# The order in which TensorE reads its streamed operand, mixed by block, in a fused attention and MLP kernel

## The chip, the cores and the metric

The kernel runs on one core of one Trainium2 chip. The metric is the device time of one execution in microseconds; a smaller number is better. Three runs of the kernel before gave a median of 866.39 us (864.64 to 867.66).

## The reference

What is computed, cut to the arithmetic, with its shapes:

```python
# q, k, v: (8, 8, 576, 64) float32;  g_norm: (64,)
kv  = np.einsum('bhsd,bhse->bhde', k, v)
out = np.einsum('bhsd,bhde->bhse', q, kv)
rms = np.sqrt(np.mean(out * out, axis=-1, keepdims=True) + 1e-06)
x   = (out / rms * g_norm).transpose(0, 2, 1, 3).reshape(4608, 512)
# w_in: (512, 2048), w_out: (2048, 512) float32
h = x @ w_in
g = np.maximum(h, 0.0) + np.log1p(np.exp(-np.abs(h)))     # softplus
return g @ w_out                                           # (4608, 512)
```

The attention is small. Nearly all work lies in the two large products, `x @ w_in` and `g @ w_out`.

## The kernel before

**Three products for one.** Inputs are float32, but TensorE reads them here as `float32r`. To keep the accuracy, each operand is split into three parts (a high part, a scaled low part and a third one that mixes both), and each large product is done as three matmuls that accumulate in the same place of `banks`, the PSUM tile. In the code `m` counts the three parts.

**Two stages.** The hidden width of 2048 is cut into 16 chunks of 128. A first stage does chunks 0 to 3 for the first four blocks of tokens, and 0 to 5 for the other eight; a block has 384 tokens, and there are 12 blocks (`n` in `step`). A wide stage does the other chunks in pairs, on blocks of 512 tokens (nine of them, `n` in `wide_step`), in two passes `ph` = 1 and 2. The list `STEPS` holds its 48 steps.

- In `step`, `mm1` (line 863) does the 12 matmuls of one chunk's first product: three parts by four blocks of the contraction (`kd`), each streaming 384 columns of `xv`. ACT takes the softplus and splits it with DVE. `mm2` (line 870) does the second product, for each of three tiles of tokens three matmuls that stream 512 columns of `w_out`.
- In `wide_step`, a pair of chunks is done by a scheme of seven half-size products instead of eight (`PRODUCTS`, functions `product` and `multiply`). Each of the seven visits has six matmuls (line 1065), three parts by two `kd`, that stream 256 columns of `dst`. The second product, `mm2` (line 1136), is done in eight visits of three matmuls that stream 512 columns of `outs[c]`.

**What sets the order.** `Plan` writes the order out ahead of time: each task carries an estimated duration and a position, and `Plan.order` places the tasks on the engines. A visit (one `product`, one `mm2`) is one task, so its matmuls follow each other on PE. The visits of L1065 and L1136 are interleaved in the wide stage, those of L863 and L870 in the first one. The plan knows nothing of the order in which a matmul reads its columns.

**The order of reading.** `from_the_end` (line 42) rewrites an operand of N columns as N/4 blocks of 4 columns, last block first. In the kernel before it is used in `product` alone, for the streamed operand and for the output in `banks`, so that each column still lands in its place. The other three lines read and write their columns in ascending order.

Of the kernel before, what the change touches and what calls it, by code (L numbers as in the profile page):

```python
# [9 lines left out]
F32R = mybir.dt.float32r  # L10
# [8 lines left out]
P = 128  # L19
# [19 lines left out]
    return x.rearrange(f"r ({' '.join(names)}) -> r {' '.join(names)}", **dict(zip(names, shape[1:])))  # L39


def from_the_end(x):

    return x.rearrange("p (b w) -> p b w", w=4)[:, ::-1]


class Slot:
# [13 lines left out]
class Plan:  # L61
# [19 lines left out]
    def slot(self, ring):  # L81
        return Slot(ring)

    def add(self, engine, ns, run, after=(), pos=0.0, take=(), give=(), size=0, behind=None, follows=None, kind="all"):
        pos, behind = round(pos, 4), None if behind is None else round(behind, 4)
        t = Task(engine, ns, run, [a for a in after if a is not None], pos, list(take), list(give), size)
        for s in t.give:
            s.readers += 1
        self.tasks.append(t)
        t.follows = follows  # L90
        t.behind = behind
        t.kind = kind
        return t
# [113 lines left out]
def kernel(  # L207
# [24 lines left out]
    nc = tc.nc  # L232
# [5 lines left out]
    KD, KF = d_model // P, d_ff // P  # L238
    NT = 384
    TB = NT // P  # L240
# [12 lines left out]
    LAST = 2  # L253
# [595 lines left out]
    def step(s):  # L849
        n, c = ORDER[s]  # L850
        cs = CHUNKS[n]
        h, g, gv = slot("h"), slot("g"), slot("gv")
        if c == cs[0]:
            sums[:] = [slot(f"s{i}") for i in range(TB)]
        xv, w_in, w_out = xv_slots[n], w_slots[0, c], w_slots[1, c]
        mine = list(sums)
        kept = c >= 4

        def mm1():
            hp = new(h, [P, NT])  # L860
            for m in range(3 * KD):
                i, kd = divmod(m, KD)
                nc.tensor.matmul(hp, lhsT=w_in.tile[:, i, kd * P:(kd + 1) * P], rhs=xv.tile[:, i, kd],  # L863
                                 start=(m == 0), stop=(m == 3 * KD - 1))

        def mm2(i):
            if c == cs[0]:
                new(mine[i], [P, d_model])
            for m in range(3):
                nc.tensor.matmul(mine[i].tile, lhsT=gv.tile[:, m, i * P:(i + 1) * P], rhs=w_out.tile[:, m],  # L870
                                 start=(c == cs[0] and m == 0), stop=(c == cs[-1] and m == 2))

        def low():
            nc.vector.tensor_tensor(out=gv.tile[:, 1], in0=g.tile, in1=gv.tile.bitcast(F32)[:, 0], op=ALU.subtract)

        def less():
            f32 = gv.tile.bitcast(F32)
            nc.vector.scalar_tensor_tensor(out=gv.tile[:, 2], in0=f32[:, 1], scalar=-RADIX, in1=f32[:, 0],
                                           op0=ALU.mult, op1=ALU.add)

        a = add("PE", 2100, mm1, x_split[n] + factors_done[0, c] + [m for _, m in mm1s[-1:]] +
                (factors_done[1, ORDER[s - 2][1]] if s > 1 else []), s, [h],
                ([xv] if c == cs[-1] else []) + ([w_in] if s == last_step[c] and c != 4 else []))
        mm1s.append((s, a))
        a = add("ACT", 490, lambda: nc.scalar.activation(new(g, [P, NT]), h.tile, func=AF.Softplus, scale=1.0 + E),  # L885
                [a], s, [g], [h])
        a = add("ACT", 530, lambda: nc.scalar.activation(new(gv, [P, 3, NT], F32R)[:, 0], g.tile, func=AF.Copy, scale=DOWN),
                [a], s, [gv])
        a = add("DVE", 570, low, [a], s, [], [g])
        a = add("DVE", 570, less, [a], s)  # L890
        for i in range(TB):
            a2 = add("PE", 700, lambda i=i: mm2(i), [a] + factors_done[1, c] + [mm2s.get(i)], s + 1.5,
                     [mine[i]] if c == cs[0] else [],
                     [gv] + ([w_out] if s == last_step[c] and not kept else []))
            mm2s[i] = a2
            if c == cs[-1]:
                leave(0, n * TB + i, mine[i], a2, s + 1.5)
# [145 lines left out]
    def wide_step(k):  # L1043
        ph, n, p = STEPS[k]
        ab, gv = slot("ab"), slot("gvp")
        b = starts[k]
# [3 lines left out]
        mine = list(wide_sums)  # L1050
        outs = [w_slots[1, c] for c in (2 * p, 2 * p + 1)]

        def place(q):
            return ab.tile[:, q // 2, q % 2 * HW:(q % 2 + 1) * HW]
# [3 lines left out]
        def product(u, q):  # L1058
            f, i = PRODUCTS[u]
            w = forms[p][f].tile  # L1060
            dst, v = unit_slots[ph, n, u]
            for m in range(3):
                for kd in range(2):
                    at = i * 2 * P + kd * P
                    nc.tensor.matmul(from_the_end(place(q)), lhsT=w[:, m, at:at + P],  # L1065
                                     rhs=from_the_end(dst.tile[:, m, v, kd] if u < 6 else dst.tile[:, m, kd]),
                                     start=(u == 0 and not m and not kd), stop=(m == 2 and kd == 1), skip_group_check=True)

        def multiply(u, q, after, pos, take=(), follows=None):
            f = PRODUCTS[u][0]  # L1070
            give = [unit_slots[ph, n, u][0]] if last else []
            if final and u in (2, 3, 5, 6):
                give.append(forms[p][f])
            return add("PE", 710, lambda: product(u, q), unit_done[ph, n, u] + forms_done[p][f] + list(after), pos, take, give,
                       follows=follows)
# [3 lines left out]
        def gt(dtype=F32):  # L1079
            if dtype not in held:  # L1080
                held[dtype] = sb.tile([P, 2, WIDE], dtype, tag=f"g{gv.place}", name=f"g{gv.place}_{dtype == F32}")
            return held[dtype]

        def gvt(m, dtype=F32):
            y = gv.tile[:, m]
            return y if dtype == F32R else y.bitcast(F32)
# [8 lines left out]
        def begin():  # L1095
            new(ab, None)
            product(0, X)
# [33 lines left out]
        def mm2(c, i):  # L1131
            fresh = first and not c and ph < LAST
            if fresh:
                new(mine[i], [P, d_model])
            for m in range(3):
                nc.tensor.matmul(mine[i].tile, lhsT=(gvt(m, F32R) if m < 2 else gt(F32R))[:, c, i * P:(i + 1) * P], rhs=outs[c].tile[:, m],  # L1136
                                 start=fresh and not m, stop=(last and c == 1 and m == 2), skip_group_check=True)

        seeds = {}
# [19 lines left out]
        for c in range(2):  # L1159
            for i in range(TW):  # L1160
                slot_pos = b + PACE + MM2[TW * c + i]
                a2 = add("PE", 700, lambda c=c, i=i: mm2(c, i),
                         [split_done[c]] + factors_done[1, 2 * p + c] + ([seeds[i]] if i in seeds and not c else []) +
                         ([before[i]] if c or not first else []), slot_pos, [mine[i]] if first and not c and ph < LAST else [], [gv] + ([outs[c]] if final else []))
                before[i] = a2
                if last and c:
                    leave(ph, TW * n + i, mine[i], a2, slot_pos)
# [98 lines left out]
```

## Time and profile before

| What | Value |
|---|---|
| median of 3 runs | 866.39 us (864.64 to 867.66) |
| the profiled execution | 864.34 us, its span 862.5 us |
| granted TensorE clock, mean | 0.999 |
| PE busy | 849.7 us, 99% of the span |
| DVE busy | 704.6 us, 82% |
| L1065, products of the wide stage | 2016 matmuls of 256 columns |
| L1136, second side of the wide stage | 1152 matmuls of 512 columns |
| L863, first product of the first stage | 768 matmuls of 384 columns |
| L870, second product of the first stage | 576 matmuls of 512 columns |

Times are of one profiled execution unless a row says otherwise. A matmul's record begins where it starts and ends where its last result is modelled to land; the records overlap, so that the distance from one start to the next is what a matmul costs in a row of them, not the length of its record. PEld is the load of the weights, which runs beside the matmuls.

### The profile page before, as it was taken

Reading aid. Unit: us, or ns where it says so; the run is one execution under the profiler, and the core shown is the slowest. Engines: PE = TensorE matmul, PEld = TensorE weight load, DVE = VectorE, ACT = ScalarE, POOL = GpSimd, SP = SyncE. Lnnn points to the kernel's source line nnn. Section 1 sums busy time; section 2 is a strip of 40 time slices with the busy share of each in tenths; the row PEclk is TensorE's granted clock in tenths of the full one; section 3 lists DMA queues with packets and bytes.
Section 4 is the critical chain, followed back from the end, with each engine's and each line's share of the span. In section 5 each row is a group of like instructions: output and inputs, shape, how many; then the busy total and the mean of one; then the engine's idle time right before and its main releaser. Section 6 shows DMA issues by size and latency. Waiting matters only on the chain.

```text
span 862.5 us, 17080 instructions
## 1 busy us (share of the span) xinstructions
PE 849.7 (99%) x6464; PEld 757.7 (88%) x6464; DVE 704.6 (82%) x995; ACT 521.2 (60%) x980; POOL 76.1 (9%) x79
## 2 busy tenths in 40 slices
PE   8899999999999999999999999999999999999998
PEld 5578888898888999999999999998999899999996
DVE  7988898888788888798888788878788766788873
ACT  6866664436354467766667665654868555566654
POOL 0342223111113300000000000000000000000000
PEclk9999999999999999999999999999999999999999
DMA  9998997779784655436645546645364753778863
GB/s 285 283 234 222 261 263 242 178 235 226 210 188 118 188 157 183 141 107 216 199 158 164 166 154 205 190 158 176 123 196 138 232 165 102 244 234 240 247 187 130
DMA packets 239778, 167.07 MB, mean 194 GB/s; under 512 B 106320, under 2 KB 198736, under 8 KB 239696
## 3 DMA queue, kind: packets, MB, share of 16 engines
q1 hardware_dynamic: 239392, 165.86, 65.7%
q8 instruction: 50, 0.82, 0.4%
q14 instruction: 32, 0.26, 0.1%
q10 hardware_dynamic: 304, 0.13, 0.1%
HBM read 112.98 MB, written 52.95 MB: 192 GB/s over the span
## 4 chain that ended last, share of the span: by engine, by line
PE 94%; DVE 1%; ACT 1%; POOL 0%; issue 0%; ACTq 0%; DVEq 0%
PE banks L1136 30%; PE banks L1065 28%; PE banks L870 16%; PE banks L863 15%; PE banks L720 2%; PE banks L696 2%; PE banks L738 0%; DVE units L643 0%; DVE half L732 0%; PE banks L1230 0%; POOL roots L728 0%; DVE units L646 0%; DVE roots L724 0%; DVE m L464 0%; ACT units L640 0%
## 5 line engine op out<-in xcount | busy, mean ns | idle before, releaser
L1136 PE MATMUL banks<-pieces,gv 128*128 128x512 f32 x768 | 238.0, 391 | 0.0
L1136 PE MATMUL banks<-pieces,g_False 128*128 128x512 f32 x384 | 149.4, 389 | 0.0
L1136 PEld LDWEIGHTS banks<-pieces,gv 128*128 128x128 f32 x768 | 132.5, 188 | 17.3
L863 PE MATMUL banks<-units,pieces 128*128 128x384 f32 x768 | 145.4, 337 | 0.0
L870 PE MATMUL banks<-pieces,gv 128*128 128x512 f32 x576 | 144.9, 396 | 0.0
L863 PEld LDWEIGHTS banks<-units,pieces 128*128 128x128 f32 x768 | 135.5, 188 | 4.9
L870 PEld LDWEIGHTS banks<-pieces,gv 128*128 128x128 f32 x576 | 106.1, 188 | 20.3
L1065 PEld LDWEIGHTS banks<-units,pieces 128*128 128x128 f32 x840 | 112.0, 188 | 6.5 <-ACT banks L1111 0.4
L1065 PE MATMUL banks<-units,pieces 128*128 128x256 f32 x840 | 116.4, 282 | 0.0
L885 ACT ACTIVATE half<-banks 128x384 f32<-128x384 f32 x64 | 31.5, 492 | 97.3 <-PE banks L863 97.1
L1126 DVE TENSOR_TENSOR gv<-g_True,gv 128x1024 fp32r<-128x1024 f32 x47 | 57.5, 1224 | 36.5 <-ACT gv L1123 36.5
L1136 PEld LDWEIGHTS banks<-pieces,g_False 128*128 128x128 f32 x384 | 72.1, 188 | 15.7
L1065 PEld LDWEIGHTS banks<-units,w 128*128 128x128 f32 x504 | 67.3, 188 | 3.7 <-ACT banks L1111 0.2
L1065 PE MATMUL banks<-units,w 128*128 128x256 f32 x504 | 70.3, 282 | 0.0
L728 POOL TENSOR_TENSOR roots<-roots,half 128x8 f32<-128x8 f32 x36 | 62.2, 1727 | 3.0
L1129 DVE SCALAR_TENSOR_TENSOR g_False<-gv 128x1024 fp32r<-128x1024 f32 x47 | 57.6, 1225 | 1.5
L1028 DVE TENSOR_TENSOR units<-loads,units 128x1024 fp32r<-128x1024 f32 x42 | 51.2, 1219 | 6.2 <-ACT units L1025 6.1
L1093 ACT ACTIVATE g_True<-banks 128x256 f32<-128x256 f32 x96 | 36.7, 383 | 31.6 <-PE banks L1065 31.0
L1115 DVE TENSOR_TENSOR g_True<-banks,g_True 128x512 f32<-128x512 f32 x48 | 33.2, 691 | 27.7 <-PE banks L1065 22.5
L930 ACT ACTIVATE m<-banks 128x512 f32<-128x512 f32 x72 | 42.1, 595 | 18.7 <-PE banks L1136 12.8
L1031 DVE SCALAR_TENSOR_TENSOR units<-units 128x1024 fp32r<-128x1024 f32 x42 | 51.4, 1224 | 1.8
L1025 ACT ACTIVATE units<-loads 128x1024 fp32r<-128x1024 f32 x42 | 44.5, 1059 | 12.4 <-PE banks L1065 8.9
(115 smaller groups left out, 1250.2 us busy)
## 6 DMA issues: line engine op xcount, KB each, us to landing
loads<-x SPq DMA_DIRECT2D x180, 128.0 KB, 2.7
part<-m SPq DMA_DIRECT2D x72, 256.0 KB, 2.9
m<-part SPq DMA_DIRECT2D x72, 256.0 KB, 3.3
loads<-form SPq DMA_DIRECT2D x45, 256.0 KB, 3.3
form<-loads SPq DMA_DIRECT2D x36, 256.0 KB, 3.1
raw<-in_moe_w_in_dram SPq DMA_DIRECT2D x16, 512.0 KB, 4.8
loads<-in_k_dram SPq DMA_DIRECT2D x32, 256.0 KB, 4.4
loads<-in_v_dram SPq DMA_DIRECT2D x32, 256.0 KB, 4.6
```

Source lines behind the costliest of these rows:

```text
L728: nc.gpsimd.tensor_tensor(out=r.tile, in0=r.tile, in1=half, op=ALU.pow)
L863: nc.tensor.matmul(hp, lhsT=w_in.tile[:, i, kd * P:(kd + 1) * P], rhs=xv.tile[:, i, kd], start=(m == 0), stop=(m == 3 * KD - 1))
L870: nc.tensor.matmul(mine[i].tile, lhsT=gv.tile[:, m, i * P:(i + 1) * P], rhs=w_out.tile[:, m], start=(c == cs[0] and m == 0), stop=(c == cs ...
L930: a = add("ACT", 690 if ph == LAST else 600, lambda: nc.scalar.activation(new(ot, [P, d_model]), bank.tile, func=AF.Copy, scale=scale if p ...
L1025: nc.scalar.activation(part_of(0, F32R), xl.tile if m > 1 else xl.tile[:, 0], func=AF.Copy, scale=DOWN)
L1028: nc.vector.tensor_tensor(out=part_of(1, F32R), in0=xl.tile if m > 1 else xl.tile[:, 0], in1=part_of(0), op=ALU.subtract)
L1031: nc.vector.scalar_tensor_tensor(out=part_of(2, F32R), in0=part_of(1), scalar=-RADIX, in1=part_of(0), op0=ALU.mult, op1=ALU.add)
L1065: nc.tensor.matmul(from_the_end(place(q)), lhsT=w[:, m, at:at + P], rhs=from_the_end(dst.tile[:, m, v, kd] if u < 6 else dst.tile[:, m, kd ...
L1093: nc.scalar.activation(dst, src, func=AF.Softplus, scale=1.0 + E)
L1126: nc.vector.tensor_tensor(out=gvt(1, F32R), in0=gt(), in1=gvt(0), op=ALU.subtract)
L1129: nc.vector.scalar_tensor_tensor(out=gt(F32R), in0=gvt(1), scalar=-RADIX, in1=gvt(0), op0=ALU.mult, op1=ALU.add)
L1136: nc.tensor.matmul(mine[i].tile, lhsT=(gvt(m, F32R) if m < 2 else gt(F32R))[:, c, i * P:(i + 1) * P], rhs=outs[c].tile[:, m], start=fresh ...
```

## The change

`from_the_end` takes the length `w` of the blocks; a length of 0 leaves the operand in ascending order. Four tables give the lengths, block by block:

- `SHORT[ph][n]`: for the six matmuls of each product visit, taken in turn. `(8, 16)` means blocks of 8 in the first, 16 in the second, 8 in the third and so on. Where all six had blocks of 4, they now have pairs, triples or one list of six lengths out of 0, 1, 2, 4, 8, 16, 32, 64 and 128.
- `LONG[n]`: for the three matmuls of a visit of the wide stage's `mm2` in pass 2: blocks of 128, none, 256, or 128 and none in turn. In pass 1 all are read in blocks of 128 from the end.
- `FIRST_SHORT[n]`: for the first and the last of the 12 matmuls of `mm1` in the first stage. The ten between stay in ascending order.
- `FIRST_LONG[n]`: for the very last matmul of a chunk's `mm2` in the first stage.

```diff
-def from_the_end(x):
-    return x.rearrange("p (b w) -> p b w", w=4)[:, ::-1]
+def from_the_end(x, w):
+    return x.rearrange("p (b w) -> p b w", w=w)[:, ::-1] if w else x
+
+SHORT = {1: [(8, 16), (16, 8, 4), (16, 8, 8), (16, 16, 8), (32, 8), (64, 8), (64, 16), (8, 1), (8, 2)],
+         2: [(128, 8), (128, 16), (16, 8, 16, 4, 16, 2), (8, 4, 16), (16, 1, 8), (16, 8), (16, 8), (16, 8), (0, 8)]}
+LONG = [(128,), (128,), (128,), (128,), (128,), (0,), (256,), (128, 0), (128,)]
+FIRST_SHORT = [(0, 0)] + [(0, 1)] * 7 + [(1, 1), (4, 1), (16, 1), (0, 2)]
+FIRST_LONG = [0, 0, 1, 4, 16, 8, 128, 64, 0, 0, 0, 2]
...
 # step, mm1
-                nc.tensor.matmul(hp, lhsT=w_in.tile[:, i, kd * P:(kd + 1) * P], rhs=xv.tile[:, i, kd],
+                w = FIRST_SHORT[n][1] if m == 3 * KD - 1 else 0 if m else FIRST_SHORT[n][0]
+                nc.tensor.matmul(from_the_end(hp, w), lhsT=w_in.tile[:, i, kd * P:(kd + 1) * P], rhs=from_the_end(xv.tile[:, i, kd], w),
...
 # step, mm2
-                nc.tensor.matmul(mine[i].tile, lhsT=gv.tile[:, m, i * P:(i + 1) * P], rhs=w_out.tile[:, m],
+                w = FIRST_LONG[n] if i == TB - 1 and m == 2 else 0
+                nc.tensor.matmul(from_the_end(mine[i].tile, w), lhsT=gv.tile[:, m, i * P:(i + 1) * P], rhs=from_the_end(w_out.tile[:, m], w),
...
 # wide_step, product
-                    nc.tensor.matmul(from_the_end(place(q)), lhsT=w[:, m, at:at + P],
-                                     rhs=from_the_end(dst.tile[:, m, v, kd] if u < 6 else dst.tile[:, m, kd]),
+                    t = SHORT[ph][n][(2 * m + kd) % len(SHORT[ph][n])]
+                    nc.tensor.matmul(from_the_end(place(q), t), lhsT=w[:, m, at:at + P],
+                                     rhs=from_the_end(dst.tile[:, m, v, kd] if u < 6 else dst.tile[:, m, kd], t),
...
 # wide_step, mm2
-                nc.tensor.matmul(mine[i].tile, lhsT=(gvt(m, F32R) if m < 2 else gt(F32R))[:, c, i * P:(i + 1) * P], rhs=outs[c].tile[:, m],
+                t = LONG[n][m % len(LONG[n])] if ph == LAST else P
+                nc.tensor.matmul(from_the_end(mine[i].tile, t), lhsT=(gvt(m, F32R) if m < 2 else gt(F32R))[:, c, i * P:(i + 1) * P],
+                                 rhs=from_the_end(outs[c].tile[:, m], t),
```

## The prediction

> **What bounds the kernel now.** I read the page from the top: busy shares, the chain that ended last, and then the waits of PE.
>
> ```profile
> span 862.5 us, 17080 instructions
> PE 849.7 (99%) x6464; PEld 757.7 (88%) x6464; DVE 704.6 (82%) x995; ACT 521.2 (60%) x980; POOL 76.1 (9%) x79
> ...
> PE 94%; DVE 1%; ACT 1%; POOL 0%; issue 0%; ACTq 0%; DVEq 0%
> PE banks L1136 30%; PE banks L1065 28%; PE banks L870 16%; PE banks L863 15%; PE banks L720 2%; PE banks L696 2%; PE banks L738 0%; DVE units L643 0%; DVE half L732 0%; PE banks L1230 0%; POOL roots L728 0%; DVE units L646 0%; DVE roots L724 0%; DVE m L464 0%; ACT units L640 0%
> ```
>
> The chain is PE for 94% of the span, and four lines hold 89% of it: the two sides of the wide stage (L1136, L1065) and the two of the first stage (L870, L863). These are exactly the four lines that the change edits. The windows by stage say the same:
>
> ```profile
> core 0: us, PE busy (x) PEld busy (x) DVE busy (x) ACT busy (x) POOL busy (x), PEclk, DMA share, GB/s
> 0.00:42.00 42.00, 34.40 (x434) 24.20 (x437) 35.20 (x64) 29.90 (x58) 8.98 (x15) 1.00 1.00 284
> 42.00:338.00 296.00, 294.52 (x2775) 261.76 (x2775) 253.71 (x435) 162.59 (x321) 67.14 (x64) 1.00 0.77 206
> 338.00:862.00 524.00, 520.78 (x3265) 471.73 (x3263) 415.68 (x498) 328.73 (x603) 0.00 (x0) 1.00 0.58 180
> ```
>
> After 42 us PE is idle for under 5 us of 820, the granted clock is 1.00, and the next engine, DVE, is busy 254 of 296 us and 416 of 524 us. So a nanosecond off a matmul's spacing moves the end, up to many microseconds, and so does one added. The question is only what an order of reading does to that spacing. A busy PE hides it, because the records of matmuls overlap; the starts show it:
>
> ```profile
> start us, us, engine line op out<-in xcount [idle before <-releaser]
> ...
> 599.74 0.88 PE L1065 MATMUL banks<-units,w 128*128 128x256 f32 x6
> 600.45 0.62 PE L1136 MATMUL banks<-pieces,gv 128*128 128x512 f32 x2
> 600.90 0.39 PE L1136 MATMUL banks<-pieces,g_False 128*128 128x512 f32 x1
> 601.13 0.62 PE L1136 MATMUL banks<-pieces,gv 128*128 128x512 f32 x2
> ```
>
> Six 256-column products take 600.45 - 599.74 = 0.71 us, 118 ns each; three 512-column ones 601.13 - 600.45 = 0.68 us, 227 ns each. The median records are 281, 334 and 389 ns for 256, 384 and 512 columns (L1065, L863, L1136), that is (389 - 281) / 256 = 0.42 ns per column. A column at that price makes 108, 162 and 216 ns; each matmul thus carries a gap of about 10 to 12 ns on top. That gap is all that an order can win: 10 ns on 2016 products and 11 ns on some 1100 long ones, 32 us at the very most.
>
> **What the trace says of the gap.** Start to start, from the start times of single records:
>
> - L863, read forward, settles at 173.4 ns; but behind L870 it begins 171, 175, 178, 185, 176, 181, 174. That is 26 ns more over seven.
> - L870, forward, settles at 227; behind L863 it begins 229, 233, 236, 224, 231, 236, 228, 233, 230, 37 ns more over nine.
> - L1136, forward: 226.9 when settled, 228.2 on average inside a visit; some visits begin 235, 231 behind L1065.
> - L1065, read from the end in blocks of 4: mean 118.5. The second, fourth and sixth intervals of a visit average 116.4; the first, third and fifth 120.2, alternating between 118 and 123.
>
> The gap is therefore not a constant: it is smallest in half of the intervals of the one line that is read backwards (116.4 - 108 = 8.4 ns, against 11 forward), and it swings for several matmuls when the shape changes. Both are small.
>
> **The change part by part.** The matmuls, their order, weights, outputs and waits stay; ACT, DVE, POOL and SP get the same rows. No wait is added. Only the patterns of the streamed operand and of the output in banks change. I count the patterns in the built program.
>
> 1. *Products, L1065.* Of 2016, 1708 get blocks of 8 to 128, 91 stay at 4, 175 get 1 or 2, 42 are read forward. Blocks longer than 4 aren't in the trace at 256 columns. The bounds are the quickest and the slowest usual interval, 115 and 123: -3.5 to +4.5 ns, or -6.0 to +7.7 us over 1708. I take halfway between the mean and the quick half (118.5 to 117.4), since a longer block lies between the two patterns seen (blocks of 4 and one whole block) and the quick half shows that the gap can shrink: -1.1 ns x 1708 = **-1.9 us**.
> 2. *Wide second side, L1136.* 1088 of 1152 get blocks of 128 (1040) or 256 (48), from the end. No 512-column read from the end is in the trace. The nearest row for a read in blocks is L1230, which reads the same 128 columns four times with a jump after each: its shortest intervals are 226 ns, so a jump per 128 columns costs nothing. For the read from the end I lean on L1065, whose gap is smaller than the forward one. Bounds: 224 (quickest in L870) and 235, against 228.1 with the last interval of a visit counted: -4.5 to +7.5 us. I take 225.6, between the quickest and the settled row: -2.5 x 1088 = **-2.7 us**.
> 3. *First stage.* The last product of L863 is changed in 60 of 64 chunks (54 to single elements, 6 to pairs) and its first in 18, the last of L870 in 38. They sit where the swings begin. All swings together are worth 3.8 x 496 = 1.9 us on L870 and 1.85 x 697 = 1.3 us on L863 (mean interval less settled one, times intervals). I take half of what the edited chunks hold: 0.9 + 0.4 = **-1.3 us**. Bounds: -2.6 us, and nothing.
> 4. *The 175 products in ones and twos, the 42 forward ones, the 91 that stay:* 0; the nearest row is the same line at 118.5. Their other end is the second rival below.
>
> Sum: -5.9 us, all on the path because PE waits for nothing there: 864.34 (the profiled execution, of which 862.5 is span) - 5.9 = 858.4. The median of the runs is 2.05 above the profiled one: 866.39 - 5.9 = **860.5**. What is late next: DVE, at 416 of 524 us, has far more room than 6 us, so nothing takes the place.
>
> The Trainium skill ("TensorE: Matmul & The Clock Gate", Back-to-back issue gap) puts a lone stream of matmuls at N/2.4 + 2.5 ns, so 109 and 216 ns. The trace differs: 118.5 and 227. If an order brought these down to the page's figures, an estimate from it is 9.5 x 1708 + 12 x 1088 = 29 us off; nothing in the trace shows such an interval.
>
> **Rivals.**
>
> *The order does nothing.* For it: settled intervals at 384 and 512 columns have the same gap to a nanosecond whatever the addresses, and 116 to 123 may be only how a steady 118.5 is dealt out. Then terms 1 and 2 vanish and 3 is lost in the noise: 866.4. Against it: the backward line's gap is smaller than the forward one. The skill's formula just named stands on this side, since it knows only N.
>
> *A change of length costs a gap (slower).* In every product visit, most neighbours now have different lengths, 8 beside 16 or 64 beside 8, where all had 4. The swings behind a change of shape show that an interval depends on what came before it. If each interval in the products goes to the slow end, 122.5, that is +4 x 1925 = +7.7 us; with -2.7 and -1.3 kept, +3.7: 870.1. It decides as soon as the mean product interval rises over 118.5 by 4.0 / 1925 = 2.1 ns, to 120.6. Against it: L1065 to L1136 and back also changes the order, and those intervals are 116.4 and 226.9, among the quickest.
>
> *Single elements are read slowly (slower).* 91 products, 60 of L863 and 4 of L870 are read element by element backwards, 84 + 12 more in pairs. If the single ones ran at half rate, they would cost 91 x 108 + 60 x 162 + 4 x 216 ns = 20.4 us; with -5.9, +14.5: 880.9. Against it: blocks of 4 have no longer records (281) than the slope from 334 and 389 gives. The Trainium skill ("PSUM — Partial Sum Buffer", Specifications) speaks for it: it gives PSUM lines of 8 bytes and says that any pattern which isn't contiguous slows matmuls significantly; the trace disagrees for blocks of 4, and no run here shows ones and twos.
>
> **How the numbers follow.** Forecast 0.51, nothing 0.19, change of length 0.17, single elements 0.11; 0.02 remains for gains beyond my bounds. A measurement of this kernel can tell 0.3% (2.6 us) from no change. Faster 0.53, same 0.19, slower 0.28. The forecast's own range is 853.4 (all three gain ends, -13.0) to 863.8; the whole range reaches up over the second rival (+7.7, half of term 2's upper end, +3.8, and -1.3 of term 3 make +10.2, so 876) and leaves out the third: 853 to 876.
>
> **What would show it.** Right: mean start to start below 118 for the products and below 227 for the long ones, no 235 at a visit's head, L870 at 227 from its first matmul in blocks 1 to 10. Wrong: blocks of the wide stage whose steps with 1 or 2 are longer by several us; the visits of the last wide block, where forward and backward alternate, out of line; or PE idle that wasn't there.

## The result and the profile after

The changed kernel takes 863.61 us (median of 20 runs, 861.93 to 866.0), the kernel before 865.19 us (20 runs). The ratio is 0.9979, with a 95% interval of 0.997 to 0.9988: faster, but by 0.2%, some 1.8 us where 5.9 were forecast. Its profiled execution took 863.30 us, 1.0 us less than the one of before. The lines move by a few numbers in the file: L863, L870, L1065 and L1136 of before are L871, L879, L1075 and L1147 of the changed kernel, and L1074 and L1146 stand for the last two in most of the experiments.

The page of the changed kernel, with its busy shares and its chain:

```profile
span 861.5 us, 17074 instructions
PE 846.8 (98%) x6464; PEld 756.4 (88%) x6464; DVE 704.5 (82%) x995; ACT 521.1 (60%) x980; POOL 76.5 (9%) x79
...
PE 94%; DMA 3%; DVE 1%; ACT 1%; SPq 1%; POOL 0%; issue 0%; POOLq 0%; DVEq 0%; ACTq 0%
PE banks L1147 31%; PE banks L1075 28%; PE banks L879 15%; PE banks L871 15%; PE banks L727 2%; PE banks L703 2%; DMA loads<-in_k_dram 1%; DMA loads<-in_v_dram 1%; DMA g<-in_v_dram 1%; DMA early<-in_q_dram 1%; PE banks L745 0%; SPq L692 0%; PE banks L783 0%; DVE half L739 0%; PE banks L1242 0%
```

The kernel is bound as before: PE is the chain, and the same four lines hold it. A point more at L1147 or less at L879 is too coarse for a change of 0.2%; the intervals below are finer. The DMA entries are the first loads, in the opening 42 us. After these, PE is idle for 5.3 us of 819, where it was idle for 4.7 of 820 (the same windows as in the prediction, columns as there):

```profile
42.00:338.00 296.00, 293.96 (x2782) 262.76 (x2783) 254.80 (x437) 164.37 (x325) 67.56 (x64) 1.00 0.78 208
338.00:861.00 523.00, 519.75 (x3258) 470.19 (x3256) 414.43 (x497) 327.42 (x601) 0.00 (x0) 1.00 0.57 179
```

Two stretches of PE's timeline show where the gain is, first of the kernel before, then of the changed one, both in the first stage (columns: start and length in us, line, operation, shapes, count):

```profile
start us, us, engine line op out<-in xcount [idle before <-releaser]
248.27 2.24 PE L870 MATMUL banks<-pieces,gv 128*128 128x512 f32 x9
250.35 2.27 PE L863 MATMUL banks<-units,pieces 128*128 128x384 f32 x12
252.46 2.24 PE L870 MATMUL banks<-pieces,gv 128*128 128x512 f32 x9
```

```profile
248.20 2.20 PE L879 MATMUL banks<-pieces,gv 128*128 128x512 f32 x9
250.24 2.25 PE L871 MATMUL banks<-units,pieces 128*128 128x384 f32 x12
252.33 2.20 PE L879 MATMUL banks<-pieces,gv 128*128 128x512 f32 x9
```

Nine matmuls of the second product took 2.08 us (231 ns each) and take 2.04 us now (227), although at most the last of the nine is read in another order. What changed is the matmul just ahead of them, the last of the first product.

With every interval from start to start taken from the single records, line by line (an interval of 260 ns or more counts as a wait and is left out of the means; the changes are differences of the sums of all intervals of a line, waits included):

| kernel | L863 | L870 | L1065 | L1136 | change of the four, us |
|---|---|---|---|---|---|
| before | 175.1 | 230.7 | 118.3 | 227.9 | |
| changed | 174.7 | 228.1 | 118.0 | 228.4 | -0.33, -1.42, -0.49, +0.49 |

The sum is -1.75 us, which is what the timed runs show. The two profiled executions differ by 1.0 us only, because in the changed one the first matmul of L871 began 0.7 us later (44.7 us after the start, 44.0 before), ahead of all edited matmuls. The expectations below give the mean of L1136 before as 227.75; by the records it is 227.9, and the changes are not touched by this.

### The profile page after: what moved, and what is told of

It is laid out like the page before. It is cut to its first block, busy times and chain, and to the rows that moved or that the text cites. A ratio compares the mean times of both kernels' runs of the same rounds, so it can differ in the third digit from the quotient of the medians.

```text
span 861.5 us, 17074 instructions
## 1 busy us (share of the span) xinstructions
PE 846.8 (98%) x6464; PEld 756.4 (88%) x6464; DVE 704.5 (82%) x995; ACT 521.1 (60%) x980; POOL 76.5 (9%) x79
## 4 chain that ended last, share of the span: by engine, by line
PE 94%; DMA 3%; DVE 1%; ACT 1%; SPq 1%; POOL 0%; issue 0%; POOLq 0%; DVEq 0%; ACTq 0%
PE banks L1147 31%; PE banks L1075 28%; PE banks L879 15%; PE banks L871 15%; PE banks L727 2%; PE banks L703 2%; DMA loads<-in_k_dram 1%; DMA loads<-in_v_dram 1%; DMA g<-in_v_dram 1%; DMA early<-in_q_dram 1%; PE banks L745 0%; SPq L692 0%; PE banks L783 0%; DVE half L739 0%; PE banks L1242 0%
## 5 line engine op out<-in xcount | busy, mean ns | idle before, releaser
L1147 PE MATMUL banks<-pieces,gv 128*128 128x512 f32 x768 | 238.2, 391 | 0.0
L1147 PE MATMUL banks<-pieces,g_False 128*128 128x512 f32 x384 | 149.9, 390 | 0.0
L1147 PEld LDWEIGHTS banks<-pieces,gv 128*128 128x128 f32 x768 | 132.8, 188 | 17.8 <-DVE banks L918 0.2
L871 PE MATMUL banks<-units,pieces 128*128 128x384 f32 x768 | 145.2, 337 | 0.0
L879 PE MATMUL banks<-pieces,gv 128*128 128x512 f32 x576 | 143.5, 394 | 0.0
L871 PEld LDWEIGHTS banks<-units,pieces 128*128 128x128 f32 x768 | 135.2, 188 | 4.6
L879 PEld LDWEIGHTS banks<-pieces,gv 128*128 128x128 f32 x576 | 106.2, 188 | 19.0
L1075 PEld LDWEIGHTS banks<-units,pieces 128*128 128x128 f32 x840 | 111.7, 188 | 6.6 <-ACT banks L1121 0.4
L1075 PE MATMUL banks<-units,pieces 128*128 128x256 f32 x840 | 116.2, 282 | 0.0
L1136 DVE TENSOR_TENSOR gv<-g_True,gv 128x1024 fp32r<-128x1024 f32 x47 | 57.5, 1223 | 37.5 <-ACT gv L1133 37.5
L1147 PEld LDWEIGHTS banks<-pieces,g_False 128*128 128x128 f32 x384 | 72.1, 188 | 15.5
L1075 PEld LDWEIGHTS banks<-units,w 128*128 128x128 f32 x504 | 67.0, 188 | 3.8 <-ACT banks L1121 0.2
L1075 PE MATMUL banks<-units,w 128*128 128x256 f32 x504 | 70.0, 281 | 0.0
```

The costliest lines, as they stand in the source:

```text
L871: nc.tensor.matmul(from_the_end(hp, w), lhsT=w_in.tile[:, i, kd * P:(kd + 1) * P], rhs=from_the_end(xv.tile[:, i, kd], w), start=(m == 0), ...
L879: nc.tensor.matmul(from_the_end(mine[i].tile, w), lhsT=gv.tile[:, m, i * P:(i + 1) * P], rhs=from_the_end(w_out.tile[:, m], w), start=(c = ...
L1075: nc.tensor.matmul(from_the_end(place(q), t), lhsT=w[:, m, at:at + P], rhs=from_the_end(dst.tile[:, m, v, kd] if u < 6 else dst.tile[:, m, ...
L1136: nc.vector.tensor_tensor(out=gvt(1, F32R), in0=gt(), in1=gvt(0), op=ALU.subtract)
L1147: nc.tensor.matmul(from_the_end(mine[i].tile, t), lhsT=(gvt(m, F32R) if m < 2 else gt(F32R))[:, c, i * P:(i + 1) * P], rhs=from_the_end(ou ...
```

## The experiments

**The three parts alone.** Each run has one part of the change and leaves the rest as before.

```diff
 # e9: wide second side alone      SHORT all (4,), FIRST_* all 0, pass 1 (128,), pass 2 LONG as changed
 # e10: products alone             SHORT as changed, the rest ascending
 # e11: first stage alone          FIRST_SHORT and FIRST_LONG as changed, SHORT all (4,), LONG 0
```

> Only the wide second side as in the changed kernel (blocks of 128 or 256 from the end); products at 4, the first stage ascending. Prediction's term 2: 225.6 ns, -2.7 us. Theory C (blocks of 128 and 256 begin at a multiple of 256 bytes, as an ascending read does, so nothing changes): 226.9 settled, 227.75 on average, the time of before within 1 us. If the changed kernel's +0.5 us on this line comes from the line itself: +0.5 us here.

> Only the products' table as in the changed kernel; the other three lines ascending. Prediction's term 1: -1.9 us. Theory C: the same sums as in the changed kernel, products -0.5 us, and the second side, though not edited, +0.5 us, because it inherits the state that the products leave; together no change within 1 us. If the second side's loss came from its own order, it is back at the 227.75 of before.

> Only the first stage's two tables as in the changed kernel. Prediction's term 3: -1.3 us. From the changed kernel's sums: L870 -1.4, L863 -0.3, so -1.7 us, nearly all of what the change brought; the wide stage as before.

| run | median, us | ratio to before | L863 | L870 | L1065 | L1136 |
|---|---|---|---|---|---|---|
| wide second side alone | 864.76 | 0.9998 (0.9988 to 1.0009) | -0.01 | -0.05 | +0.06 | -0.06 |
| products alone | 864.87 | 0.9995 (0.9984 to 1.0006) | +0.03 | +0.03 | -0.43 | +0.49 |
| first stage alone | 863.30 | 0.9977 (0.9967 to 0.9987) | -0.29 | -1.52 | +0.11 | -0.06 |

(The last four columns are changes in us against before, by intervals.) The parts add up. The long matmuls' own order is worth nothing; their loss of 0.49 us in the changed kernel appears in full when only the products are edited, so it is handed on by the products. The first stage makes the whole gain.

The blocks of the first stage tell its two edits apart. In blocks 1 to 7 the last matmul of the first product is read in single elements and the first stays ascending: L879's mean falls to 227.0 in block 6 and 227.7 in block 7 (230.6 and 231.0 before; by less in blocks 1 to 5), while L871 stays at 175.2 and 175.1. In blocks 8 and 9 the first matmul is edited too, and L871 falls to 173.9 and 173.8 (174.9 and 175.2 before).

**What the products' order is worth.** Three kernels differ only in the lengths of the products' blocks; the other lines are ascending as before.

```diff
-SHORT: all (4,)
+e1: all (0,)        e3: all (16, 8)        e7: all (8, 16)
```

> All four lines read in ascending order, the products too (before: blocks of 4 from the end). Theory A (a matmul's interval depends on the order of reading, and a product that is read as its neighbours are pays the full gap): products at 120.0 ns start to start where the kernel before has 118.5, so 2016 x 1.5 = +3.0 us; long ones unchanged. Theory B (order does nothing, the swings come from the shapes alone): same time within 1 us, same swings at the same places.

> Only the products changed, all to blocks of 16 and 8 in turn; the long ones ascending. Theory A (16 first, then 8 settles into visits of 700 ns, as in wide blocks 5 to 7 of pass 2): products 116.7 instead of 118.5, 336 visits x 10 ns = -3.4 us, and no visits of the second side that begin at 235. Rival (those blocks were quick because of their place in pass 2, or because of the reading of the second side there): pass 1 stays at 118 to 119, about -1 us.

> As the run with products in blocks of 16 and 8 in turn, but 8 first and 16 second, as wide block 0 of pass 1 has it. If only the mixture of lengths mattered: visits of 700 ns, the same time as with 16 first. Theory A (what matters is from where to where the reading jumps between neighbours, and this differs with the place in the visit): visits of 720 ns, products at 120 instead of 117, +6 us against 16 first, about 867; and visits of the second side that begin at 231 to 237.

| products read | median, us | ratio to before | L1065 | L1136 | visits of at most 702 ns |
|---|---|---|---|---|---|
| blocks of 4 (before) | 865.15 | | 118.3 | 227.9 | 0 of 336 |
| ascending | 869.99 | 1.0051 (1.0036 to 1.0065) | 119.3 | 230.0 | none |
| 16, 8 | 861.12 | 0.9949 (0.9932 to 0.9966) | 117.0 | 227.1 | 93% |
| 8, 16 | 869.09 | 1.0041 (1.0026 to 1.0056) | 118.7 | 231.3 | 32% |

The order that comes 16 first is 0.9% faster than the same lengths with 8 first. Block lengths as such, and mixing as such, explain neither. With ascending products the second side, not edited, lost 2.35 us, more than the products' own 2.07; its expectation had left it unchanged. A stretch of the wide stage in both, 16 first and then 8 first:

```profile
560.98 0.86 PE L1074 MATMUL banks<-units,pieces 128*128 128x256 f32 x6
561.68 0.62 PE L1146 MATMUL banks<-pieces,gv 128*128 128x512 f32 x2
562.14 0.39 PE L1146 MATMUL banks<-pieces,g_False 128*128 128x512 f32 x1
562.36 0.86 PE L1074 MATMUL banks<-units,pieces 128*128 128x256 f32 x6
```

```profile
563.29 0.88 PE L1074 MATMUL banks<-units,pieces 128*128 128x256 f32 x6
564.01 0.63 PE L1146 MATMUL banks<-pieces,gv 128*128 128x512 f32 x2
564.48 0.40 PE L1146 MATMUL banks<-pieces,g_False 128*128 128x512 f32 x1
564.71 0.62 PE L1146 MATMUL banks<-pieces,gv 128*128 128x512 f32 x2
```

In the first a visit of products lasts 0.70 us and the second-side visit behind it 0.68; in the second 0.72 and 0.70. The second side is read ascending in both. Single intervals tell two rhythms apart: 117, 117, 116 again and again (700 ns a visit), or 119 to 121 (720 ns a visit). The kernel before sits in a third, between them (707 to 712 ns in 331 of 336 visits). Behind the quick visits of the run with 16 first the long matmuls take 227 ns; with 8 first they mostly take 230 to 236, whether the visit ahead took 700 ns or 720.

A rhythm tends to run on. With 8 first all visits are read alike, and yet some are quick and some not: directly behind a quick product visit, 63 of 63 were quick; directly behind one that was not, 1 of 105; behind the second side, 44 of 168. That fits a rhythm that is carried from one visit into the next.

**Reading or writing.** The pair 16 and 8 was applied to one side of each product only.

```diff
 # e5: only what is read
-matmul(from_the_end(place(q), t), ..., rhs=from_the_end(dst..., t))
+matmul(place(q), ..., rhs=from_the_end(dst..., t))
 # e6: only what is written
+matmul(from_the_end(place(q), t), ..., rhs=dst...)
```

In both, the columns land in other places than they should, so the output is not the kernel's; the count and the length of the matmuls stay.

> Products in blocks of 16 and 8 in turn in what they read from SBUF; what they write to banks ascends, so that columns land in other places and the output isn't the reference's. Theory A (the reading of SBUF decides): visits of 700 ns as with both, about 861. Rival (the writing to PSUM decides): 720 ns as with ascending products, about 870.

> The mirror of the run before: products read in ascending order, and write to banks in blocks of 16 and 8 in turn from the end; columns land in other places and the output isn't the reference's. Theory A (the reading decides): 720 ns a visit, about 870. Rival (the writing decides): 700 ns, about 861. If both come out between, both sides count.

Read alone: 861.18 us, 0.995 (0.9934 to 0.9966), products at 116.9. Written alone: 869.47 us, 1.0045 (1.0029 to 1.0061), products at 119.3. These are the numbers of 16, 8 and of ascending. The reading of SBUF decides, and the order of writing PSUM is free in the orders tried.

**PE by itself.** Groups of matmuls ahead of the kernel's work, when nothing else uses its operands. Within a group each matmul takes the next of 12 weight tiles and of three places of the stream.

```diff
+for i in range(36):
+    nc.tensor.matmul(from_the_end(banks[:W, 0, :N], b), lhsT=lab_w[:, wi:wi + W],
+                     rhs=from_the_end(lab_x[:, off + step:off + step + N], a), start=(i == 0), stop=(i == 35))
```

> The kernel before with groups of 36 extra matmuls ahead of its work, each group alike, on tiles of the identity, read from the profile by start-to-start time; its whole time is of no interest. They vary the width of the weights (128, 64 or 32 columns), the length of the stream (512, 384, 256), the blocks (1 to 256 from the end), pairs, read alone or written alone from the end, and where the streamed operand begins against the weights (0 to 128 words). Theory A1 (the gap of a settled matmul is the load of the next weights taking SBUF turns from the stream, one turn per line of 4 words, so 32 turns of 0.42 ns = 13.3 ns for 128 columns): 512 columns take 227 ns with 128-column weights, 220 with 64, 217 with 32. Theory A2 (a fixed change of weights): 227 with all three. Both theories: single elements are no slower than blocks of 4 (under 125 ns at 256 columns).

The timeline of that run; each row is a group, and the distance to the next row's start, divided by 36, is the interval:

```profile
19.16 8.32 PE L1225 MATMUL banks<-pieces 128*128 128x512 f32 x36
27.32 8.44 PE L1229 MATMUL banks<-pieces 128*64 128x512 f32 x36
35.60 8.50 PE L1233 MATMUL banks<-pieces 128*32 128x512 f32 x36
43.94 6.43 PE L1237 MATMUL banks<-pieces 128*128 128x384 f32 x36
...
73.37 4.42 PE L1261 MATMUL banks<-pieces 128*128 128x256 f32 x36
77.63 4.48 PE L1265 MATMUL banks<-pieces 128*128 128x256 f32 x36
81.94 4.41 PE L1269 MATMUL banks<-pieces 128*128 128x256 f32 x36
...
149.37 4.48 PE L1317 MATMUL banks<-pieces 128*128 128x256 f32 x36
153.69 4.37 PE L1321 MATMUL banks<-pieces 128*128 128x256 f32 x36
157.89 4.36 PE L1325 MATMUL banks<-pieces 128*128 128x256 f32 x36
162.09 4.36 PE L1329 MATMUL banks<-pieces 128*128 128x256 f32 x36
...
182.79 8.40 PE L1341 MATMUL banks<-pieces 128*128 128x512 f32 x36
191.03 8.53 PE L1345 MATMUL banks<-pieces 128*128 128x512 f32 x36
199.39 8.33 PE L1349 MATMUL banks<-pieces 128*128 128x512 f32 x36
207.56 4.48 PE L1353 MATMUL banks<-pieces 128*128 128x256 f32 x36
211.87 12.70 PE L1357 MATMUL banks<-pieces 128*128 128x384 f32 x63
224.41 12.54 PE L1361 MATMUL banks<-pieces 128*128 128x384 f32 x63
236.79 8.56 PE L1365 MATMUL banks<-pieces 128*128 128x256 f32 x54
```

- Weights of 128, 64 and 32 columns (L1225, L1229, L1233): 226.7, 230.0 and 231.7 ns. At 512 columns fewer weights make it longer, not shorter (at 256 columns 64 make it shorter, 113.4 ns). Both A1 (220 and 217) and A2 (227 throughout) fall.
- Blocks at 256 columns, over the second half of a group: 1, 2 and 4 all 118.5; 8 is 120.0 (L1265); 16 is 117.9; 32 is 118.9; 64, 128 and ascending 120.0 to 120.2. Single elements are not slow. A longer block is not quicker.
- 8, 16 (L1317) 120.0; 16, 8 (L1321) 116.7; none, 8 (L1325) 116.7, and 64, 8 behind it (L1329) the same. Beside PE and its loads of weights no engine was busy for more than 0.1 us from 19 to 262 us, and the DMA moved 1 GB/s, so the rhythms belong to PE and its reading. The three quick groups stand one behind the other, so the second and third may owe it to the first.
- A stream of 512 columns that begins 4, 16 or 32 words (of 4 bytes) from its tile's start: 231.4, 228.8 (L1341), 231.9 (L1345); 0, 64 or 128 words: 226.7 (L1349).
- At 512 columns, blocks of 128 and 256 give 226.7, the ascending number, and blocks of 4 and 8 give 233.4.
- Twelve matmuls of 384 and nine of 512 in turn (L1357) repeat the swing of the first stage (229, 233, 236 and on); with 4 first and 1 last among the twelve (L1361) it is gone (226 to 228 throughout the nine).
- Six matmuls of 256 and three of 512 in turn, as in the wide stage: with blocks of 4 the nine are as in the kernel before (707 ns for the six, then 235, 231, 227). With 16, 8 and long ones in blocks of 256 they are not quick, as they are in the kernel, but take 718 to 720 ns and then 234, 236, 224.

A second run of groups asked what the start and what the order inside contribute.

> More groups of 36 matmuls ahead of the kernel before: at 256 columns ascending reads that begin 4, 8, 16 or 32 words earlier, alone and in pairs; all pairs of blocks out of 0, 4, 8, 16 and 32 at 256, 512 and 384 columns; and the pair of 16 and 8 with one weight tile throughout or with weights that begin one tile later. Theory C (only the place of the first word within 256 bytes counts, against that of the weights; blocks of w from the end begin 4w bytes early): early starts give the same as blocks, 118.5, 120.0, 117.9, 118.9 and 116.7 for the pair 16 and 8. Theory D (the order inside counts): early starts give 120 or something else of their own. For the order within the pair: if 8 before 16 is slow because of the weights' place, weights one tile later swap the two (16, 8 at 120 and 8, 16 at 116.7); if a state is only carried on from the group before, they don't swap. I expect pairs at 512 and 384 columns not under 226.7 and 173.3.

Three stretches of it (its line numbers are its own: L1325 and L1565 are both 16, 8, L1565 with weights one tile later, L1561 is 8, 16):

```profile
124.84 4.48 PE L1325 MATMUL banks<-pieces 128*128 128x256 f32 x36
129.16 4.40 PE L1329 MATMUL banks<-pieces 128*128 128x256 f32 x36
...
531.02 4.48 PE L1561 MATMUL banks<-pieces 128*128 128x256 f32 x36
535.33 4.37 PE L1565 MATMUL banks<-pieces 128*128 128x256 f32 x36
539.53 4.48 PE L1569 MATMUL banks<-pieces 128*128 128x256 f32 x36
```

Ascending reads that begin 4, 8, 16 and 32 words early took 117.4, 118.6, 117.8 and 118.8; blocks of that length 118.3, 120.0, 117.9 and 118.9. At 16 and 32 the two agree, as C says, and at 4 and 8 they do not, as D says: the start of the stream moves the interval off 120 by itself, and the order inside counts as well. The pair of early starts, 16 then 8, took 118.2; the pair of an ascending read and one that begins 8 words early took 116.7, the quick number with no order changed at all.

The pair 16, 8 took 119.9 this time, 119.9 with one weight tile throughout and 116.7 with weights one tile later, while 8, 16 stayed at 120 in all three: no swap. None, 8 took 118.5, and the pairs 4, 16 and 16, 4 were quick (116.7). The same stream can thus run in either rhythm. Both times that 16, 8 was quick, in this run and in the first, the group ahead of it was 8, 16; both times that it took 119.9 it was another. That fits a rhythm which depends on what ran ahead, in four cases, of which two had other weights. Of all pairs of 0, 4, 8, 16 and 32 at 512 and 384 columns none was under 226.7 and 173.3, the ascending ones.

**The place in SBUF, with no order changed.**

```diff
-    SHIFT = 64
+    SHIFT = 32        # e8_shift32; in e8_shift128: 128
```

> The kernel before with all its orders as they were; the gap in SBUF between the units and the weights' pieces is 32 words instead of 64, so that streams and weights begin 128 bytes apart within 256 instead of at the same place. Theory C: no order of reading changes, yet intervals do: 512 columns go from 227 to some 232 (as with 32 words in the first lab run), so 1728 x 5 = +9 us, products and L863 by a few ns too; 870 to 880. Theory D: same time as before.

> The same with a gap of 128 words, a whole multiple of 256 bytes more than before. Theory C: same time as before within 1 us and the same swings. If the place counts beyond 256 bytes: any other time.

32 words: 875.79 us, 1.0117 (1.0097 to 1.0136); L863 176.2, L870 232.5, L1065 119.8, L1136 232.4. 128 words: 865.57 us, 1.0 (0.9988 to 1.0011), intervals as before to 0.1 ns. Moving everything behind the gap by 128 bytes costs 10 us, some six times what the studied change brought, and moving it by 256 bytes from where it was costs nothing. In L863 and L1065 the streams lie ahead of the gap and stayed, and the weights moved: +0.6 and +3.1 us by intervals. In L870 and L1136 the streams moved and the weights stayed: +1.0 and +5.2 us. So it is not the stream's place alone, unless the products' loss was handed on to them by the second side; no run moved one line's operands alone.

**The first stage in one way, and all together.**

```diff
+e2: FIRST_SHORT all (4, 1), FIRST_LONG all 0; SHORT all (4,), LONG 0
+e4: FIRST_SHORT all (4, 1), FIRST_LONG all 0; SHORT all (16, 8), LONG all (256,)
```

> Only the first stage changed, and the same way in all its blocks: in each chunk's first product the first matmul in blocks of 4 and the last in single elements, as block 9 of the changed kernel has it. Theory A (a swing is set off by the order in which the last and first matmul of a visit are read, and runs on until something stops it): L870 falls from 231 to 227 ns and L863 from 175.2 to 173.9, 576 x 4 + 768 x 1.3 = -3.3 us. Theory B (order does nothing): no change. A rival of A, that single elements are slow, would show in the last interval of each first product: 173 if not, over 300 if so.

> The best pieces of the changed kernel in all blocks: products 16 and 8 in turn, the wide second side in blocks of 256 from the end, the first stage with blocks of 4 first and single elements last. Theory A: products 116.7, wide second side 226.8, L870 227, L863 173.9: -3.4 - 1.3 - 2.3 - 1.0 = -8 us against before, about 857. Rival (the states depend on what came before, and don't add up): under -4 us.

The first stage so: 863.07 us, 0.9974 (0.9961 to 0.9986), L863 174.4 and L870 227.8, -2.4 us by intervals, where 3.3 were expected. Together: 860.18 us, 0.9929 (0.9909 to 0.995), -0.73, -1.61, -2.64 and -1.09 us on the four lines, -6.1 us in sum: less than the 8 expected, more than the rival's 4. This has the lowest median of all versions run, 0.7% under before; that it beats the run with 16, 8 alone (861.12) is shown by the intervals only, as the two ratios' 95% intervals overlap. It gets about what the prediction had forecast for the mixture, by one setting in every block instead of eighteen lists.

## Why the prediction was right or wrong

**Where it looked was right.** The four lines bind, a nanosecond of interval goes to the end (-1.75 us by intervals, some 1.8 by the timed runs), and the direction held. The sum did not: -1.9, -2.7 and -1.3 us were forecast, and -0.49, +0.49 and -1.75 came. That 863.61 us still lies in the forecast's own range, 853.4 to 863.8, is luck: the kernel before took 865.19 us beside it, 1.2 less than the 866.39 that the range was counted from. Of the signs of being right only L870 showed one, and in part: its means are 226.7 to 228.0 in blocks 6 to 10, and 228.4 to 229.8 in blocks 1 to 5. The products stayed at 118.0, the long ones rose to 228.4, and visits still begin at 235.

**Term 1 (products, -1.9 us) failed at its choice of value**: it measured -0.49 (-0.43 alone). The step "a longer block lies between the two patterns seen" took the length for the quantity that counts. It does not order the intervals at all: 118.5, 120.0, 117.9, 118.9 for 4, 8, 16, 32. What the trace of before did show, and the prediction listed without using it, was a rhythm of four intervals (118, 116, 123, 116) that runs on across visits. In the changed kernel 28% of the visits fell into the quick rhythm, 87 of these 94 in six blocks: with 64, 8 or 128, 8 or 16, 8 or none, 8 the blocks' means are 116.3 to 117.1; with 8, 4, 16 and 16, 8, 4 or with 8, 16 or 128, 16 they are 118.9 to 119.2, above the 118.3 of before (visits counted to blocks in the order of their starts).

**Term 2 (second side, -2.7 us) failed in its mechanism**: by its own order it is worth -0.06 us. The step "for the read from the end I lean on L1065, whose gap is smaller than the forward one" doesn't carry over to 512 columns: the groups give 226.7 ns for blocks of 128, of 256 and for ascending reads alike. This fits that such blocks start a whole number of 256 bytes from where an ascending read starts, but no run tells this reason from others. The row of L1230 bears less than the prediction took from it: of its 16 intervals under 260 ns three are at 224 to 227 and thirteen at 229 to 236; that a jump per 128 columns costs nothing was right, as the groups show. The +0.49 us measured comes from the products, since it is there when they alone are edited. Behind product visits of at most 702 ns, a visit of L1147 takes 682 ns on average (48 of them), behind those of 703 to 713 ns 691 (95), behind longer ones 695 (22); before, it took 689 behind all. These nearly cancel (+0.07 us); the rest lies in the long visits further behind, whose intervals rise from 226.7 to 227.3 ns (653 of them).

**Term 3 (first stage, -1.3 us) was right, and a little small**: -1.75 (-1.81 alone). The edited matmul is the one that the swing starts from, and changing it stops the swing for the nine that follow in blocks 6 to 10. The share taken, half, was the error on L870: 1.42 of the 1.9 us came back. On L863 0.33 us came for 0.4.

**The rivals.** *The order does nothing* holds for the wide second side and for no other line. *A change of length costs a gap* is refuted as stated: 16, 8 changes the length at each step and is the quickest; 8, 16 does too and is slower than before (118.7 for 118.3 ns, and 231.3 for 227.9 behind it); ascending throughout, with no change of length among the products, is slower still (119.3). *Single elements are slow* is refuted: 118.5 ns at 256 columns, as for 2 and 4, and 173.7 as the last of the twelve in the first stage (mean of 53 free intervals, the run with 4 and 1). The Trainium skill's rule on PSUM ("PSUM — Partial Sum Buffer", Specifications: patterns that aren't contiguous slow matmuls significantly) is not borne out: with only the writes in blocks of 16 and 8 the kernel takes 869.47 us, with ascending writes and reads 869.99, and a group that writes single elements from the end and reads ascending takes 120.0 ns, as with ascending writes. The formula that the prediction took from the Trainium skill for the isolated gap ("TensorE: Matmul & The Clock Gate", Back-to-back issue gap) holds the length alone; here the same 256 columns take 116.7 or 120.0 ns.

**What stays open.** Why there are several rhythms, and what selects one: the start of the stream within 256 bytes, the order inside and what ran ahead all count, the width of the weights counts, their place may, and no single rule fitted the groups. That a product visit's length predicts the next long visit is not general either: with 8, 16 everywhere, long visits behind quick product visits took 699 ns, behind the others 701. Nor did the groups that imitate the wide stage with 16, 8 fall into the rhythm that the kernel has with it.

## What to carry to other kernels

Where PE is the chain, compare start-to-start intervals of single matmuls, visit by visit; a spread of 3 to 10 ns between equal matmuls is a rhythm that can be changed by trial; between the two orders of 16 and 8 it is worth 0.9% here. Before changing orders of reading, try where the weights and the streams lie within 256 bytes: that alone moved this kernel by 1.2%. Test one order in every block: with a table that mixes them blocks at 116.3 to 117.1 ns and blocks at 118.9 to 119.2 come out as one mean of 118.0, and a rhythm can run on from one visit into the next.

## What was not expected of the hardware

- The same read can take two intervals, and what ran ahead goes with which: the same 36 matmuls in blocks of 16 and 8 ran at 116.7 or at 119.9 ns in two runs whose programs differ in the groups ahead (and which were on two chips). Within one run, 16, 8 took both numbers too, and with 8 first a visit directly behind a quick one was quick in 63 of 63 cases.
- Single elements, pairs and blocks of 4 from the end give the same 118.5 ns; the Trainium skill ("SBUF — State Buffer", Specifications) gives SBUF lines of 16 bytes, and within such a line the order makes no difference here.
- The Trainium skill ("TensorE: Matmul & The Clock Gate", Step-by-step: what each phase is for) says that loading the next weights doesn't take SBUF read bandwidth from the running matmul. Here the same stream took another interval with weights of another width (next point), so the two are not independent, whatever links them. The products also went from 118.3 to 119.8 ns when their weights moved by 128 bytes and their streams did not, but the second side's streams moved in that run too.
- Weights of 64 columns in place of 128 made 512 columns slower (230.0 for 226.7 ns) and 256 columns quicker (113.4 for 120); at 384 it changed nothing (173.2 for 173.3).
